# Heads grouped by halves of the rows and sums of exponentials on GpSimd, in an attention and feed-forward kernel ordered by a written list

## The chip, the core and the metric

The kernel runs on one core of a Trainium2 chip. The metric is the device time of one execution in microseconds (us), lower being better. Several runs are given by their median. The engines are called PE (the matrix engine; its weight loads are shown apart as PEld), DVE (the vector engine), ACT (the scalar engine), POOL (GpSimd) and SP (the queue that issues the stores).

## What is computed

The reference has two parts. The first is an attention over 32 memory slots, for 8 batches, 8 heads, 576 tokens and a head size of 64. The second is a feed-forward product, whose input is the attention's output with the heads side by side.

```python
a = exp(phi - max(phi, axis=2));  a = a / (sum(a, axis=2) + 1e-9)
k_m = einsum('bhsm,bhsd->bhmd', a, k);  v_m = einsum('bhsm,bhsd->bhmd', a, v)
attn = softmax(q @ k_m^T / 8);  x = attn @ v_m          # heads merged: (4608, 512)
out = ((x @ w_a) * (x @ w_b)) @ w_out                    # 512 -> 1536 -> 512
```

The sum below a slot's exponentials is a sum over tokens: 32 slots, each with its own sum, for each head and batch.

## The kernel before

**Layout.** A batch's q, k, v and phi are loaded as 128 partitions by four slabs (`hp`). Partitions 0 to 63 of slab `hp` hold head 2·hp, partitions 64 to 127 head 2·hp+1, and each partition has nine tokens of its head. So a head is named by the half of the rows that it lies in (`r`, 0 or 1) and its slab. A group `g` is four heads, `j` = 0 to 3, whose 32 slots each lie side by side in 128 partitions. `head(g, j)` says which heads make a group: it crosses the halves, so that each group takes two heads from either half.

**Batches 2 to 7.** `exp0` and `exp1` (L260) take exponentials of phi on ACT, two slabs each. `kv` (`kv_sums`, L286) multiplies the exponentials with k, v and a block of ones in 72 products of 64 rows, 32 columns and 192 moving columns, on eight tiles of the array at once. The block of ones gives each slot's sum. `km` (`take_kv`, L313 and L318) divides by the sums into a tile of six 128x128 squares (`rep`), in which the means stand repeated, since the scores and the folds read them from the rows in which the head's data lie. `kvt` (L326, L327) turns the six squares on PE and copies them out. `sc` (L375) makes the scores from the turned means and the transposed q (`qt0` to `qt3`, L269). `e0` and `e1` take their exponentials, `den`, `nr` or `ed`, `sm`, `tn`, `ad` normalise. `v0` to `v2` (`fold`, L447) multiply the value means into w_a and w_b, and `x0` to `x2` (L460) copy these out.

**Batches 0 and 1** do the same in smaller steps (`ks`, `kt`, `vs`, `vt`, `s`, `hv`, `hx`, L340 to L361), because their inputs still arrive.

**Feed-forward.** `a` and `b` (`up_half`, L621) are two products each with 288 moving columns: batch, one of twelve blocks of the 1536 columns, half of the tokens. ACT copies the first (L625), DVE multiplies it with the second (L628). The down product is made for two blocks of 128 tokens at once by seven products instead of eight, from sums of the inputs (`h` on POOL, `g` on DVE, L534) and of the weights (`T` on POOL, `V` on DVE, L517). A `d` with a number is that many of its 756 matmuls of 256 columns (L550).

**Order.** Nothing is reordered by the compiler. A string, `PLAN`, lists all steps, and every engine runs its own instructions in the order in which the list issues them. `F` and `f` with a number are matmuls of 512 and 128 columns on zeros that keep PE busy. `p`, `k`, `v`, `q`, `w` and `o` are loads, all issued from POOL: phi, k, v and q of a batch, columns of w_a and w_b, rows of w_out. `M` is a POOL memset of the block of ones of odd batches, `O` fills the matrix that `den` multiplies with.

Tiles for phi and q have two buffers each, so batch b+2's phi takes the place of batch b's. k and v have one tile for even batches and one for odd.

Of the kernel before, what the change touches and what calls it, by code (L numbers as in the profile page):

```python
# [13 lines left out]
P = 128  # L14
# [11 lines left out]
f3 F1 O 0exp0 f1 f1 F2 p1 f2 f6 F7 w0:256 f2 f1 k1 f1 F3 0exp1 F5 f2 0qt0 q1.0 0ks0 0ks1 F5 0kt0 0qt1 M F2 0s0  # L26
w256:512 0qt2 0kt1 0e0 0den00 0qt3 0s1 0e1 F4 0den01 1exp0 0vs0 q1.1 0vt0 v1 0vs1 1exp1 F6 0nr00 0den10 0vt1
0den11 0hv0a 0hx0a 0nr10 0hv0b 0hx0b 0nr11 a0.1.0 b0.1.0 a0.0.0 F4 0nr01 1ks0 1ks1 b0.0.0 0hv1a 0hx1a 1kt0 1kt1
1qt0 1qt1 a0.0.1 a0.2.1 F1 b0.0.1 1s0 a0.1.1 0hv1b 1qt2 1qt3 0hx1b 1s1 1e0 1e1 b0.2.1 1den0 a0.2.0 b0.1.1 b0.2.0
1den1 1vs1 1vs0 1vt1 1nr0 1vt0 1nr1 a0.3.1 a0.3.0 1hv1b 1hx1b 1hv0b 1hv0a 1hx0a w512:1024 1hx0b b0.3.1 b0.3.0  # L30
1hv1a 0v1a 1hx1a 0x1a a1.0.0 a1.1.1 a1.1.0 a1.0.1 b1.0.0 b1.1.1 b1.1.0 a1.3.0 b1.0.1 a1.3.1 b1.3.0 b1.3.1 a0.5.0
0v1b 1v1a w1024:1536 0x1b 1x1a a1.2.0 1v1b 0v2a 1x1b o1 0x2a a0.7.1 b0.5.0 b1.2.0 b0.7.1 a0.7.0 b0.7.0 o5 a1.5.0
a1.2.1 b1.2.1 b1.5.0 a0.4.0 a0.6.0 b0.4.0 a0.4.1 a1.4.0 b0.6.0 b1.4.0 a0.9.1 0v2b 1v2b 1v2a 0x2b 1x2b a1.5.1
b0.4.1 1x2a b0.9.1 a0.8.0 a1.4.1 b1.5.1 o2 a0.5.1 a0.6.1 b0.8.0 a0.9.0 b0.6.1 b0.9.0 b1.4.1 a1.7.1 b0.5.1 b1.7.1
a0.8.1 b0.8.1 o0 a1.7.0 a0.10.0 b1.7.0 b0.10.0 a0.11.0 a1.9.0 o3 o4 b0.11.0 g0.0 b1.9.0 a1.6.1 k2 a1.6.0 p2 h0.3
a0.11.1 b1.6.1 b0.11.1 a1.8.1 a0.10.1 b1.6.0 v2 b1.8.1 g0.1 T01 a1.8.0 T00 V20 q2 T21 d1 2exp0 a1.9.1 d3 b0.10.1
p3 a1.10.0 d2 V10 g0.2 V11 d1 b1.9.1 2exp1 d1 a1.11.1 k3 d1 q3 T31 T30 d1 b1.10.0 b1.8.0 d1 b1.11.1 d4 h1.0 d2
2kv d4 2km d3 a1.11.0 d10 a1.10.1 2qt0 3exp0 d1 2kvt d2 h1.1 d1 2qt1 d12 2qt2 d3 2qt3 b1.10.1 g1.2 b1.11.0 v3 d1
2sc 2e0 d1 g1.3 d3 g2.0 d3 2e1 d1 2den0 h2.1 d8 p4 d8 2nr0 2den1 g2.2 2v0 2x0a 2x0b d2 2nr1 d10 2v1 d5 2x1a 3qt0
d3 g2.3 d3 2x1b d1 a2.3.0 a2.2.0 b2.3.0 b2.2.0 q4 k4 v4 a2.5.0 3exp1 b2.5.0 d2 3qt1 d4 a2.0.0 b2.0.0 d3 h3.0  # L40
a2.1.0 a2.4.0 2v2 3kv 3qt3 2x2a 3qt2 b2.1.0 2x2b d2 a2.11.1 a2.6.0 d4 3km a2.8.0 d1 q5 b2.4.0 d3 b2.6.0 d2 4exp0
d5 b2.11.1 d5 h3.1 d2 b2.8.0 a2.11.0 3kvt d2 a2.8.1 a2.7.1 b2.8.1 d2 a2.9.0 b2.7.1 3sc 3e1 3e0 g3.3 d1 b2.11.0
4qt0 a2.7.0 d2 a2.5.1 b2.5.1 b2.7.0 h3.2 3den0 d1 3nr0 4qt3 d1 b2.9.0 d2 a2.0.1 4qt2 a2.10.0 b2.0.1 p5 a2.4.1
b2.10.0 d1 k5 a2.10.1 d3 b2.10.1 d3 h4.0 4exp1 d1 a2.2.1 b2.4.1 3den1 d4 3v1 3x1a 4kv 3v0b 3x1b d3 3x0b d1 3nr1
d6 4km0 h4.1 a2.6.1 b2.2.1 a2.9.1 4qt1 a2.1.1 3v0a 3v2 d1 3x0a d2 3x2a d2 b2.6.1 3x2b d4 a3.9.0 d4 a3.5.0 d2
4km1 h4.2 b2.9.1 d1 a2.3.1 4kvt d1 b2.1.1 d1 b2.3.1 d2 5qt0 4sc a3.11.0 d1 h4.3 b3.5.0 5qt2 d5 4e1 d1 4e0 d1 v5
d6 b3.9.0 a3.0.0 g5.0 d1 h5.1 d3 4ed b3.11.0 d1 a3.3.0 d2 a3.10.1 b3.0.0 h5.2 5exp0 4sm0 q6 a3.1.0 d1 b3.3.0 d4
a3.3.1 d2 p6 d2 b3.10.1 a3.8.1 h5.3 d1 b3.3.1 b3.1.0 a3.6.0 b3.6.0 a3.7.0 a3.10.0 b3.8.1 d1 a3.1.1 b3.7.0 5qt1
d2 a3.8.0 a3.2.0 b3.10.0 d3 5exp1 a3.4.0 d1 b3.8.0 b3.1.1 d2 b3.2.0 k6 b3.4.0 4v0a 5kv 4x0a d1 a3.2.1 5km0
a3.4.1 5km1 d3 h6.0 h6.1 b3.2.1 d1 a3.9.1 d3 a3.5.1 d1 b3.4.1 b3.9.1 d5 4v0b 4x0b 4tn0 4v1 d1 h6.3 d3 4x1a d1  # L50
4x1b d2 a3.11.1 5kvt d1 p7 4sm1 a3.7.1 h6.2 d1 v6 d3 a3.6.1 d2 b3.5.1 b3.11.1 d1 5qt3 4v2 d4 4tn1 a3.0.1 d7 4x2a
4ad 6exp0 d1 b3.0.1 d6 4x2b b3.7.1 a4.11.0 b3.6.1 d1 a4.9.0 6exp1 d1 6qt0 b4.11.0 a4.7.0 a4.4.0 d4 b4.9.0 k7 d1
5sc 5e1 d1 5e0 d1 a4.0.0 d1 b4.4.0 d1 b4.0.0 a4.2.0 b4.2.0 d1 b4.7.0 d3 6qt1 d2 a4.4.1 d2 q7 a4.1.1 b4.4.1 5v0
5x0a 5x0b 6kv 5v1 h7.0 5x1a d3 6km0 a4.10.1 d1 5ed 6km1 d2 h7.3 h7.1 b4.1.1 h7.2 g8.0 d1 5x1b d2 h8.1 d1 a4.6.1
d4 b4.6.1 d4 a4.8.0 a4.5.0 5sm0 d1 v7 d1 h8.2 b4.10.1 a4.8.1 b4.8.0 a4.3.1 b4.5.0 d2 6qt3 d7 5v2 d2 5x2a d2
a4.1.0 d2 b4.3.1 7qt0 a4.3.0 d1 5x2b d1 b4.8.1 d1 7qt2 d1 b4.3.0 a4.5.1 d2 a4.10.0 b4.1.0 d2 6kvt 7exp0 d2 5tn0
d3 5sm1 a4.0.1 b4.5.1 d1 6qt2 d2 b4.0.1 d1 a4.6.0 d3 a4.7.1 d5 h8.3 d1 b4.10.0 d1 7exp1 d2 5tn1 d1 7qt1 a4.11.1
d3 6sc d5 6e1 d5 a4.2.1 d1 b4.7.1 d1 b4.6.0 5ad d1 a4.9.1 d1 h9.0 d1 b4.2.1 d3 6e0 b4.11.1 d1 b4.9.1 d1 a5.2.0
d1 a5.2.1 6ed g9.1 d1 b5.2.0 6v0a 6x0a 6v0b 7kv 6x0b b5.2.1 a5.11.0 b5.11.0 a5.8.0 a5.9.0 b5.8.0 h9.2 d1 7km0 d1
a5.3.0 d1 h9.3 d2 b5.9.0 b5.3.0 d2 a5.6.0 d1 g10.0 d1 h10.1 b5.6.0 a5.3.1 h10.3 d4 b5.3.1 d2 a5.1.0 d5 7qt3 d4  # L60
a5.7.0 d1 7km1 a5.7.1 b5.7.1 d9 b5.7.0 a5.5.0 d3 b5.1.0 d4 6sm0 b5.5.0 d3 a5.0.0 a5.1.1 d1 a5.10.0 d1 b5.0.0
7kvt d3 a5.0.1 d2 h10.2 b5.1.1 b5.0.1 d6 b5.10.0 a5.11.1 a5.10.1 6sm1 a5.4.0 d2 6v1 b5.10.1 6x1a d3 b5.4.0 d2
6x1b d1 b5.11.1 d1 a5.5.1 a5.9.1 6v2 6x2b b5.5.1 d1 6tn1 d1 a5.8.1 d1 6tn0 a5.6.1 d1 6x2a a5.4.1 d1 6ad b5.9.1
d4 7sc d1 7e1 7e0 b5.6.1 d2 b5.4.1 b5.8.1 a6.7.0 d1 7ed a6.9.0 7v0a 7v1 g11.0 d2 7x1a d2 g11.1 d2 a6.10.0 h11.3
h11.2 d1 h12.0 d3 7x0a 7sm0 a6.0.0 d2 b6.7.0 d2 b6.10.0 d4 b6.9.0 d5 a6.3.0 d7 a6.11.0 b6.11.0 b6.0.0 d1 a6.2.0
d5 b6.2.0 d1 a6.8.0 d1 b6.3.0 d1 7x1b d1 a6.5.0 h12.1 a6.10.1 b6.5.0 d4 7sm1 d4 h12.2 d3 a6.6.1 d2 g12.3 d3
b6.8.0 d6 a6.4.1 d3 b6.4.1 a6.9.1 d2 7tn1 b6.10.1 d1 7tn0 d3 7ad d2 b6.6.1 a6.2.1 a6.3.1 d1 a6.1.0 d1 b6.3.1
b6.2.1 d2 b6.9.1 d5 a6.8.1 a6.4.0 b6.1.0 b6.8.1 a6.11.1 b6.4.0 a6.6.0 b6.6.0 h13.0 a6.1.1 h13.1 a6.5.1 b6.11.1
d1 b6.5.1 d1 7v0b 7v2 d1 7x0b 7x2a a6.0.1 b6.1.1 d1 7x2b b6.0.1 d1 g13.2 d1 a6.7.1 d2 a7.11.0 d5 a7.6.0 a7.7.0
d7 g13.3 d1 b6.7.1 b7.6.0 b7.11.0 a7.0.0 d1 b7.7.0 d2 a7.2.0 d1 b7.0.0 d10 a7.1.0 a7.4.1 a7.3.0 d1 b7.2.0 b7.3.0  # L70
b7.1.0 d1 a7.10.1 a7.4.0 h14.0 h14.3 d7 b7.4.1 d2 a7.5.0 a7.10.0 g14.1 b7.5.0 d1 b7.4.0 b7.10.1 a7.5.1 a7.3.1
b7.5.1 d1 b7.10.0 a7.8.0 d1 a7.9.1 b7.3.1 d1 h14.2 a7.1.1 d1 b7.8.0 b7.9.1 a7.8.1 a7.9.0 d2 b7.9.0 d3 h15.0 d1
h15.1 d2 a7.2.1 b7.1.1 d3 a7.7.1 d15 b7.8.1 d3 g15.2 d4 a7.0.1 g15.3 d11 b7.0.1 d3 b7.2.1 d1 a7.11.1 d3 b7.7.1
d1 a7.6.1 d2 b7.11.1 d10 b7.6.1 g16.0 d6 g16.1 d5 g16.2 d1 g17.0 d11 h16.3 d8 h17.1 d24 h17.3 d13 g17.2 d28
# [4 lines left out]
def kernel(  # L79
# [167 lines left out]
    def head(g, j):  # L247

        jj = j ^ g
        return jj % 2, 2 * g + jj // 2  # L250

    def units(b):

        u = {}
# [16 lines left out]
        def slot_sums(z):  # L271
            if z == 0:
                t["es"] = kvs[b][:, 2, 0, 0:2 * NHP * M].bitcast(F32).rearrange("p (c m) -> p c m", m=M)
            nc.vector.tensor_reduce(out=t["es"][:, 2 * z:2 * z + 2], in_=t["exp"][:, 2 * z:2 * z + 2].rearrange("p c i m -> p c m i"),
                                    axis=mybir.AxisListType.X, op=ALU.add)
# [30 lines left out]
        def take_kv(gs=range(2)):  # L306

            if gs[0] == 0:
                t["rep"] = mid.tile([P, 6, P], F16, name="rep")
                t["rphi"] = small.tile([P, 2], F32, name="rphi")  # L310
            for g in gs:
                pkv, bank = t["pkv"][g]
                nc.vector.reciprocal(out=t["rphi"][:, g:g + 1], in_=pkv[:, 2 * D:2 * D + 1])  # L313
                km = pkv[:, 0:D].rearrange("p (d e) -> p e d", e=2).unsqueeze(2).to_broadcast([P, 2, 4, 32])
                vm = pkv[:, D:2 * D].unsqueeze(1).to_broadcast([P, 2, D])
                for out, x in ((t["rep"][:, 2 * g:2 * g + 2].rearrange("p e (z d) -> p e z d", z=4), km),
                               (t["rep"][:, 4 + g].rearrange("p (z d) -> p z d", z=2), vm)):
                    nc.vector.tensor_scalar(out=out, in0=x, scalar1=t["rphi"][:, g:g + 1], scalar2=None, op0=ALU.mult)  # L318
                banks.free(bank)

        def kv_transpose():
# [3 lines left out]
            for x in range(6):  # L325
                nc.tensor.transpose(out=pT[:, x, :], in_=t["rep"][:, x], identity=ident)  # L326
# [136 lines left out]
        def one(f, *a):  # L463
            return lambda: f(*a)
# [221 lines left out]
```

## Time and profile before

| | |
|---|---|
| time, median of 3 runs | 237.14 us (237.03 to 237.19) |
| time of the profiled execution | 237.06 us |
| its span | 235.4 us |
| PE busy | 226.6 us, 96% |
| DVE busy | 186.9 us, 79% |
| ACT busy | 152.6 us, 65% |
| POOL busy | 132.0 us, 56% |

The span is what the profiler saw of the program, from its first instruction to its last. Some 1.7 us of the execution's time lie outside it. Busy shares are means over the whole span. A PE matmul's busy time contains the latency of its result, and matmuls overlap; the distance from one start to the next says more of its cost.

### The profile page before, as it was taken

What the parts mean: (1) busy time and instruction counts of PE and PEld (TensorE: products, weight loads), DVE (VectorE), ACT (ScalarE), POOL (GpSimd) and SP (SyncE); (2) the same over time, 40 slices, a digit from 0 to 9 for tenths busy, and PEclk for the clock granted to TensorE, in tenths of its full rate; (3) what the DMA queues carried; (4) which work ended last, traced back from release to release, by engine and by line L of the source; (5) the groups of instructions that cost most, each with busy time, mean ns of one, the idle gap of its engine ahead of it and who ended that gap; (6) DMA issues with size and microseconds to landing.
All of it is one profiled execution on the core that took longest, in us unless ns stands there. A gap on an engine that the chain in (4) does not pass through costs nothing.

```text
span 235.4 us, 7727 instructions
## 1 busy us (share of the span) xinstructions
PE 226.6 (96%) x3075; PEld 171.4 (73%) x3075; DVE 186.9 (79%) x454; ACT 152.6 (65%) x398; POOL 132.0 (56%) x117
## 2 busy tenths in 40 slices
PE   7988899999999999999999999999999999999993
PEld 4534466788877887888777778788668887888882
DVE  4536699999988889898897998987798687776842
ACT  2265598875697699667787856754884757464330
POOL 6784423895695647776979380665209205535251
PEclk9999999999999999999999999999999999999999
DMA  6999999999999979399699582303030412041264
GB/s 232 235 252 203 207 207 207 205 259 258 214 249 214 198 170 238 66 176 214 117 227 206 133 138 54 92 1 92 1 76 16 92 45 49 1 93 43 57 148 111
DMA packets 25748, 34.12 MB, mean 145 GB/s; under 512 B 2000, under 2 KB 19792, under 8 KB 25712
## 3 DMA queue, kind: packets, MB, share of 16 engines
q0 software_dynamic: 19248, 23.14, 54.0%
q1 hardware_dynamic: 5952, 9.70, 15.6%
q10 hardware_dynamic: 512, 0.79, 1.0%
q8 instruction: 24, 0.39, 0.6%
q14 instruction: 12, 0.10, 0.1%
HBM read 42.47 MB, written 9.44 MB: 221 GB/s over the span
## 4 chain that ended last, share of the span: by engine, by line
PE 86%; DMA 7%; POOL 3%; DVE 1%; issue 0%
PE py L550 21%; PE pb L621 20%; PE pa L621 20%; PE pv L550 10%; PE pva L447 5%; PE px L550 5%; DMA q_sb<-in_q_dram 5%; DMA ht<-in_k_dram 2%; PE pkv L286 2%; PE pscore L375 1%; POOL kv_sb L639 1%; PE pT L326 1%; PE pD L398 1%; POOL wa_sb L159 1%; DVE kv_sb L217 1%; POOL wb_sb L160 1%
## 5 line engine op out<-in xcount | busy, mean ns | idle before, releaser
L625 ACT CAST a_sb<-pa 128x288 f16<-128x288 f32 x192 | 72.3, 407 | 38.1 <-PE pa L621 30.6
L628 DVE TENSOR_TENSOR ht<-a_sb,pb 128x288 f16<-128x288 f16 x192 | 80.1, 447 | 19.6 <-PE pb L621 12.0
L621 PEld LDWEIGHTS <-vab 128*128 128x128 f16 x768 | 73.8, 98 | 19.1 <-issue 3.0
L621 PE MATMUL pb<-A,vab 128*128 128x288 f16 x384 | 71.9, 286 | 0.0
L621 PE MATMUL pa<-A,vab 128*128 128x288 f16 x384 | 71.3, 286 | 0.6 <-DVE A L409 0.4
L534 POOL TENSOR_TENSOR h_sums<-ht 128x768 f16<-128x768 f16 x22 | 36.0, 1640 | 36.5 <-DVE ht L628 36.4
L550 PEld LDWEIGHTS <-h_sums 128*128 128x128 f16 x432 | 41.8, 98 | 9.0 <-issue 1.5
L550 PEld LDWEIGHTS <-ht 128*128 128x128 f16 x324 | 31.0, 98 | 8.5 <-issue 3.5
L460 ACT CAST vab<-pva 128x512 f16<-128x512 f32 (+1 forms) x60 | 31.3, 570 | 7.2 <-PE pva L447 6.8
L550 PE MATMUL py<-w_sums,h_sums 128*128 128x256 f16 x216 | 35.4, 273 | 0.0
L534 POOL TENSOR_TENSOR h_sums<-h_sums,ht 128x768 f16<-128x768 f16 x13 | 21.3, 1639 | 15.1 <-DVE h_sums L534 7.1
L460 DVE CAST vab<-pva 128x512 f16<-128x512 f32 (+1 forms) x44 | 26.8, 635 | 2.9 <-PE pva L447 2.8
L534 POOL TENSOR_TENSOR h_sums<-ht,h_sums 128x768 f16<-128x768 f16 x11 | 18.1, 1643 | 11.0 <-PE pa L621 5.9
L550 PE MATMUL pv<-w_sums,h_sums 128*128 128x256 f16 x108 | 19.3, 273 | 0.0
L557 ACT ACTIVATE u<-py 128x256 f32<-128x256 f32 x36 | 14.0, 390 | 8.1 <-PE py L550 6.2
L550 PE MATMUL px<-wo_sb,ht 128*128 128x256 f16 x108 | 19.0, 273 | 0.0
L550 PE MATMUL py<-wo_sb,ht 128*128 128x256 f16 x108 | 18.9, 273 | 0.0
L550 PE MATMUL py<-w_sums,ht 128*128 128x256 f16 x108 | 18.5, 273 | 0.0
L550 PE MATMUL pv<-wo_sb,h_sums 128*128 128x256 f16 x108 | 18.5, 273 | 0.0
L269 DVE STREAM_TRANSPOSE qT<-q_sb 128x288 f32<-128x288 f32 x32 | 14.5, 465 | 2.1 <-DMA q_sb<-in_q_dram 2.1
L260 ACT ACTIVATE exp_sb<-phi_sb 128x576 f16<-128x576 f32 x16 | 10.8, 687 | 6.0 <-DMA phi_sb<-in_phi_dram 6.0
L211 PE MATMUL pw<-warm 128*128 128x512 f16 (+1 forms) x59 | 13.2, 382 | 1.3 <-DVE warm L180 1.3
(69 smaller groups left out, 247.5 us busy)
## 6 DMA issues: line engine op xcount, KB each, us to landing
out_dram<-o_sb SPq DMA_DIRECT2D x68, 128.0 KB, 2.4
phi_sb<-in_phi_dram POOLq DMA_DIRECT2D x8, 576.0 KB, 7.1
kv_sb<-in_v_dram POOLq DMA_DIRECT2D x8, 576.0 KB, 9.2
kv_sb<-in_k_dram POOLq DMA_DIRECT2D x7, 576.0 KB, 9.9
q_sb<-in_q_dram POOLq DMA_DIRECT2D x6, 576.0 KB, 10.7
wo_sb<-in_moe_w_out_dram POOLq DMA_DIRECT2D x6, 256.0 KB, 15.8
q_sb<-in_q_dram POOLq DMA_DIRECT2D x4, 288.0 KB, 9.7
wa_sb<-in_moe_w_a_dram POOLq DMA_DIRECT2D x2, 512.0 KB, 15.3
```

What stands on the lines that cost most here:

```text
L211: nc.tensor.matmul(pw[:, :cols], warm[:, :P], warm[:, :cols], start=True, stop=True)
L260: nc.scalar.activation(out=t["exp"][:, 2 * z:2 * z + 2, :, :], in_=phis[b][:, 2 * z:2 * z + 2, :].rearrange("p c (i m) -> p c i m", m=M), ...
L269: nc.vector.transpose(out=t["qT"][:, hp, :].bitcast(F32), in_=qs[b][:, hp, :].bitcast(F32))
L286: nc.tensor.matmul(t["pkv"][g][0][32 * j:32 * j + 32, 0:n], t["exp"][64 * r:64 * r + 64, hp, i, :], kvs[b][64 * r:64 * r + 64, 0:3 - given ...
L447: nc.tensor.matmul(t["pva", lo, z][g][0][32 * j:32 * j + 32, 0:hi - lo], t["kvT"][64 * r:64 * r + 64, 4 + g, M * j:M * j + M], w_sbs[z][64 ...
L460: engine_copy(out=vabs[b][z][:, g, lo:hi], in_=pva[:, 0:hi - lo])
L534: engine.tensor_tensor(out=out, in0=in0, in1=in1, op=op)
L550: nc.tensor.matmul(po, lhs[:, i], rhs[:, i], start=first and i == 0, stop=i == KH - 1, skip_group_check=not first)
L557: nc.scalar.mul(out=x, in_=po, mul=scale)
L621: nc.tensor.matmul(ps, vabs[b][x][:, g, P * i:P * (i + 1)], attn[b][:, g, HALF * hf:HALF * (hf + 1)], start=(g == 0), stop=(g == 1))
L625: nc.scalar.copy(out=a_sbs[b, i, hf], in_=ps)
L628: nc.vector.tensor_tensor(out=ht[:, i, t0:t0 + HALF], in0=a_sbs.pop((b, i, hf)), in1=ps, op=ALU.mult)
```

## The change

Four things change.

1. From batch 2 on a group is made by `straight`: group 0 is the four heads of partitions 0 to 63, group 1 those of partitions 64 to 127. Both groups then share three squares, one group in either half, where there were six. `take_kv` writes half the columns, `kv_transpose` makes three products and a copy of 384 columns. Batches 0 and 1 keep `crossed`, and their turned means move to a pool of their own.
2. The block of ones leaves the product of batches 2 to 7. A step `ps0` (`slot_sums`) adds the exponentials over the nine tokens of each partition in four POOL instructions of 512, 256, 128 and 128 elements, in 32-bit, into the phi tile that the exponentials came from. Eight small products of 32-bit operands, with one moving column, finish the sum over partitions at the end of `kv_sums` (the branch `given`, which stood in the kernel but was not used).
3. `slot_sums` as it stood (two DVE reductions into the block of ones) is gone; no list called it.
4. The list is written anew. The number of `a`, `b` and `d` steps is the same. POOL's `h` go from 46 to 42 and DVE's `g` from 26 to 30, `T` from 5 to 6 and `V` from 3 to 2. `F` go from 40 to 47 and `f` from 19 to 6.

```diff
-    def head(g, j):
+    def crossed(g, j):
         jj = j ^ g
         return jj % 2, 2 * g + jj // 2
+    def straight(g, j):
+        return g, j
     def units(b):
+        side = b < 2
+        head = crossed if side else straight
...
-        def slot_sums(z):
-            if z == 0:
-                t["es"] = kvs[b][:, 2, 0, 0:2 * NHP * M].bitcast(F32).rearrange("p (c m) -> p c m", m=M)
-            nc.vector.tensor_reduce(...)
+        def slot_sums():
+            e = t["exp"]
+            f = phis[b].rearrange("p c (i m) -> p c i m", m=M)
+            for out, in0, in1 in ((f[:, :, 0:4], e[:, :, 0:4], e[:, :, 4:8]), (f[:, :, 0:2], f[:, :, 0:2], f[:, :, 2:4]),
+                                  (f[:, :, 0], f[:, :, 0], f[:, :, 1]), (f[:, :, 0], f[:, :, 0], e[:, :, 8])):
+                nc.gpsimd.tensor_tensor(out=out, in0=in0, in1=in1, op=ALU.add)
+            t["es"] = f[:, :, 0]
...
         def take_kv(gs=range(2)):
-                t["rep"] = mid.tile([P, 6, P], F16, name="rep")
+                t["rep"] = mid.tile([P, 3, P], F16, name="rep")
...
-                km = pkv[:, 0:D].rearrange("p (d e) -> p e d", e=2).unsqueeze(2).to_broadcast([P, 2, 4, 32])
-                vm = pkv[:, D:2 * D].unsqueeze(1).to_broadcast([P, 2, D])
-                for out, x in ((t["rep"][:, 2 * g:2 * g + 2].rearrange("p e (z d) -> p e z d", z=4), km),
-                               (t["rep"][:, 4 + g].rearrange("p (z d) -> p z d", z=2), vm)):
+                km = pkv[:, 0:D].rearrange("p (d e) -> p e d", e=2).unsqueeze(2).to_broadcast([P, 2, 2, 32])
+                half = slice(D * g, D * (g + 1))
+                for out, x in ((t["rep"][:, 0:2, half].rearrange("p e (z d) -> p e z d", z=2), km),
+                               (t["rep"][:, 2, half], pkv[:, D:2 * D])):
...
         def kv_transpose():
-            t["kvT"] = mid.tile([P, 6, P], F16, name="kvT")
-            pT = banks.tile([P, 6, P], F16, name="pT")
-            for x in range(6):
+            t["kvT"] = mid.tile([P, 3, P], F16, name="kvT")
+            pT = banks.tile([P, 3, P], F16, name="pT")
+            for x in range(3):
...
         def sums(g, x):
-                t["kvT"] = mid.tile([P, 6, P], F16, name="kvT")
+                t["kvT"] = consts.tile([P, 6, P], F16, name=f"kvT{b}")
...
         def scores(gs):
-                                t["kvT"][row:row + 32, 2 * g + dh, M * j:M * j + M],
+                                t["kvT"][row:row + 32, (2 * g if side else 0) + dh, M * j:M * j + M],
...
         def fold(lo, hi, zs):
-                            t["kvT"][64 * r:64 * r + 64, 4 + g, M * j:M * j + M],
+                            t["kvT"][64 * r:64 * r + 64, 4 + g if side else 2, M * j:M * j + M],
...
-            u[f"ps{z}"] = one(slot_sums, z)
+        u["ps0"] = slot_sums
```

Of the new list, the start and the stretches in which batches 2 to 4 have their sums:

```diff
+p1 F2 F2 M f2 0exp0 F2 F4 O F3 f3 F2 F6 f1 0exp1 0ks0 0ks1 F3 0kt0 0qt0 0qt1 0s0 k1 F1 0qt2 0e0 w0:256 F8 0kt1
+0vs0 0qt3 0den00 0vs1 q1.0 1exp0 0s1 w256:512 F3 0vt0 0vt1 0e1 0den10 0nr00 0den01 F2 0den11 q1.1 v1 0nr01 1exp1
+1ks0 0hv0a 0nr10 0hx0a 1kt0 0nr11 1ks1 F5 0hv0b a0.1.0 1qt0 a0.0.1 1qt1 w512:1024 0hx0b 1s0 0hv1a 0hx1a a0.0.0
+b0.1.0 b0.0.0 1kt1 b0.0.1 0hv1b 1e0 0hx1b 1qt3 1den0 1qt2 a0.1.1 a0.2.0 b0.1.1 a0.3.1 1nr0 1s1 1e1 b0.2.0 a0.2.1
+a0.3.0 b0.2.1 1den1 b0.3.0 1vs1 1vs0 1vt1 1vt0 w1024:1536 1nr1 b0.3.1 1hv0b 1hv0a 1hv1b 1hx1b 1hx0a 1hv1a 0v1a
...
+b1.9.0 a1.8.1 a1.6.0 b1.6.0 2exp0 a0.10.1 d1 b1.8.1 a1.10.0 v2 g0.1 d1 T01 a1.9.1 a1.8.0 V20 T00 d4 g0.2 V11
+b0.10.1 q2 d1 T21 b1.10.0 d2 2exp1 p3 d1 T10 d1 a1.11.1 d1 b1.9.1 d3 q3 2ps0 b1.8.0 d2 b1.11.1 d7 k3 d1 T30 d2
+T31 d1 g1.0 2kv 2km d1 F4 d5 2qt0 2qt3 2qt1 2qt2 a1.10.1 g1.1 v3 d2 3exp0 a1.11.0 2kvt b1.11.0 b1.10.1 d2 g1.2
+d16 2sc d1 q4 d1 g1.3 2e0 2e1 d9 g2.0 d1 2den0 2den1 d1 g2.1 3exp1 2nr0 2nr1 d1 g2.3 d7 g2.2 d1 2v0 d6 2x0b d1
+p4 d1 3qt0 d6 3qt2 d2 2x0a d1 2v1 2x1a d8 2x1b a2.2.0 3ps0 3qt3 a2.3.0 b2.3.0 a2.0.0 h3.0 d2 b2.2.0 d1 k4 d1
+b2.0.0 d6 h3.1 d3 2v2 3kv 2x2a 2x2b d1 a2.8.0 d1 a2.5.0 a2.4.0 d2 v4 3qt1 3km p5 b2.5.0 b2.8.0 d1 a2.1.0 q5 d7
...
+a2.7.1 a2.7.0 4qt3 d1 4qt2 4exp0 d6 4exp1 d1 b2.8.1 b2.7.0 b2.7.1 d1 3den0 a2.0.1 h3.3 d3 b2.0.1 4qt1 a2.11.0 d1
+a2.1.1 d2 3nr0 a2.10.0 b2.11.0 d2 b2.10.0 d2 3den1 d2 a2.10.1 d2 q6 g4.0 3v1 3x1b 4ps0 d1 b2.1.1 d3 a2.4.1 d1
+a2.6.1 h4.1 d1 b2.10.1 a2.2.1 d1 3x1a d6 v5 d1 a2.9.1 3v0b 3x0b 4kv 4km0 d1 h4.2 d5 4km1 d1 3v2 3v0a 3nr1 3x2a
```

The start of the list before, for comparison:

```diff
-f3 F1 O 0exp0 f1 f1 F2 p1 f2 f6 F7 w0:256 f2 f1 k1 f1 F3 0exp1 F5 f2 0qt0 q1.0 0ks0 0ks1 F5 0kt0 0qt1 M F2 0s0
-w256:512 0qt2 0kt1 0e0 0den00 0qt3 0s1 0e1 F4 0den01 1exp0 0vs0 q1.1 0vt0 v1 0vs1 1exp1 F6 0nr00 0den10 0vt1
-0den11 0hv0a 0hx0a 0nr10 0hv0b 0hx0b 0nr11 a0.1.0 b0.1.0 a0.0.0 F4 0nr01 1ks0 1ks1 b0.0.0 0hv1a 0hx1a 1kt0 1kt1
-1qt0 1qt1 a0.0.1 a0.2.1 F1 b0.0.1 1s0 a0.1.1 0hv1b 1qt2 1qt3 0hx1b 1s1 1e0 1e1 b0.2.1 1den0 a0.2.0 b0.1.1 b0.2.0
-1den1 1vs1 1vs0 1vt1 1nr0 1vt0 1nr1 a0.3.1 a0.3.0 1hv1b 1hx1b 1hv0b 1hv0a 1hx0a w512:1024 1hx0b b0.3.1 b0.3.0
```

## The prediction

> **What bounds the kernel now.** I read the page's busy shares and slices first, then the table of stretches, then the chain of waits, and last single steps in the order of time.
>
> ```profile
> PE 226.6 (96%) x3075; PEld 171.4 (73%) x3075; DVE 186.9 (79%) x454; ACT 152.6 (65%) x398; POOL 132.0 (56%) x117
> PEclk9999999999999999999999999999999999999999
> ```
>
> ```profile
> 24.00:30.00 6.00, 5.33 (x93) 2.76 (x97) 3.92 (x11) 3.90 (x13) 2.10 (x3) 1.00 1.22 207
> 30.00:42.00 12.00, 11.82 (x219) 7.91 (x220) 11.88 (x32) 11.11 (x31) 3.60 (x5) 1.00 1.24 207
> 42.00:60.00 18.00, 18.00 (x237) 14.19 (x235) 17.27 (x44) 12.64 (x35) 14.53 (x12) 1.00 1.19 240
> 60.00:100.00 40.00, 40.00 (x634) 31.17 (x632) 35.28 (x86) 32.17 (x84) 26.97 (x23) 1.00 0.94 192
> 150.00:200.00 50.00, 50.00 (x589) 39.14 (x588) 41.59 (x97) 33.68 (x89) 22.04 (x15) 1.00 0.21 49
> ```
>
> The columns are the stretch, its length, the busy time of PE, PEld, DVE, ACT and POOL, the granted clock, the DMA share and GB/s. From 42 us on PE has no hole, at the full clock (1.00). So from there any start-to-start time that leaves PE shortens the run, and any that is added lengthens it; other engines count only if PE comes to wait for them. POOL is busy 14.53 of 18 us from 42 to 60, which is where it may become late, and only 22.04 of 50 from 150 on. Before 42 us DMA is full (share over 1.2), and the start is a matter of landings:
>
> ```profile
> 11.78 2.03 POOL kv_sb L639
> 15.17 11.87 DMA q_sb<-in_q_dram
> 29.97 0.79 PE pk L340 x72
> ```
>
> The chain puts 2.03 us on the memset `M`. It should not be believed: the load behind it landed 11.87 us after its issue, since the queue was full of earlier bytes. `M`'s move to an earlier place is worth nothing, and `p1`'s too (its bytes follow v's in either list).
>
> Prices of single steps, start to start:
>
> ```profile
> 56.22 0.94 PE L286 MATMUL pkv<-kv_sb,exp_sb 64*32 64x192 f16 x72
> 57.09 0.28 PE L550 MATMUL py<-w_sums,h_sums 128*128 128x256 f16 x1
> 59.56 0.50 PE L326 MATMUL pT<-ident,rep 128*128 128x128 f16 x6
> 59.89 0.27 PE L550 MATMUL px<-wo_sb,ht 128*128 128x256 f16 x1
> 60.00 0.27 PE L550 MATMUL py<-w_sums,ht 128*128 128x256 f16 x1
> 13.81 1.04 PE L211 MATMUL pw<-warm 128*128 128x512 f16 x4
> 14.69 0.29 PE L398 MATMUL pD<-E,ones 128*128 128x288 f16 x1
> ```
>
> So a `kv` takes 0.87 us, six turning products 0.33, a down matmul of 256 columns 0.11 (0.43 ns a column), four fills of 512 columns 0.88. By the same count an up half is 0.245.
>
> **Part by part.** All sums are against the profiled execution, 237.06 us, 0.08 below the median of 237.14.
>
> *Turning.* Three products fewer, 0.33/2 = 0.17, six batches: 1.0 us off PE. The shorter DVE work (rows of 484 and 342 ns become like the 342 and 284 ns rows, the copy of 555 ns becomes shorter; some 0.6 us a batch) lies beside PE and is set at nothing; were DVE the bound it would be a gain.
>
> *Width.* 72 products on eight tiles are nine waves; 64 columns fewer are 64 x 0.43 = 27 ns a wave, 0.25 us a batch: 1.5 us off PE.
>
> *Eight small products.* No row shows 32-bit operands. Below, at the spacing of the other `kv` products (0.87/72 = 12 ns) with half of it hidden: 0.05 us a batch. Above, one after another like the turning products (56 ns): 0.45. I take 0.2, nearer to the `kv` row, since they too lie on eight tiles, but with a weight load that nothing hides. Six batches: 1.2 us on PE (0.3 to 2.7).
>
> The Trainium skill, "FP8 and Floating Point Precision", TensorE Precision Notes, says that true 32-bit products take four passes. By that the eight would be 32 small ones, and as the 32 score products take 0.41 us here, the sum would be 1.3 us later; no run here shows it yet.
>
> *Grouping by halves.* Scores and folds keep their number, tiles and columns, and either order uses all tiles at once. Nothing.
>
> *Sums on POOL.* 1024 elements a batch. POOL's two-input rows (768 elements 1640 ns, 576 1279, 640 1265) give 2.0 to 2.2 ns an element, 2.2 us, and four starts at 0.08 make some 2.4. Bounds: 2.0, and 4.0 if 32-bit results cost more. In all 14.4 us on POOL, while four `h` leave it and a `T` comes (net -4.9): 132 becomes about 141 of 235.
>
> The Trainium skill, "GPSIMD Engine Reference", Engine selection, speaks against this part: two-input elementwise work and sums along the free dimension belong on VectorE, GpSimd being about 2x slower. Here it is 3x (`h_sums` takes 1640 ns on POOL, 545 on DVE). By the rule one would lose 14.4 us of engine time; as neither engine is the bound, I count only PE's waits.
>
> PE waits if `ps0` is late, for the small products stand in PE's order before all that follows. Counting PE's steps in the list: from `2exp1` to `2kv` four up halves and 20 down matmuls, 3.2 us, and 0.6 of `kv` itself; against that the exponentials (0.69), some 0.1 to 0.5 of ACT's backlog and 2.4: 0.2 to 0.6 spare. Batch 3: 8.3 us of steps from `2nr0` on, against 1.3 us of lag as before, two `nr` (2.6), `p4` (0.8), 2.4: 1.8 spare with `kv`'s 0.6. Batch 4: 6.0 from `3nr0`, against 1.7 of lag, 1.3, `q6` 0.75, 2.4: 0.5 spare. Batches 5 to 7: over 1.5. So nothing, up to the point where a sum takes about 2.9 us.
>
> phi's loads `p4` to `p7` now wait on POOL's queue for the sums and the small products of two batches before. Those lie 1 us (`p5`) to over 7 us earlier in the list, so nothing. `q`, `k` and `v` change places by one load, 1.5 to 3 us in a stream that is 10 to 30 us ahead of use after 65 us: nothing.
>
> *A fill at 58 us.* `F4` stands in the new list behind `2km`: 0.9 us on PE, certain. It covers a wait rather than making one: `T30` and `T31` now come behind `ps0` on POOL, ending some 7.1 to 7.5 us after `2exp1`, and PE's 40th down matmul, which needs `T31`, has 7.1 us of steps before it with the fill. Left out, PE would wait about as long.
>
> *One more changeover* between tile shapes (`3v1` now stands apart): 0.15.
>
> *The start.* The weights w0:256 land 2.8 us later (k1 goes ahead of them), w256:512 (24.3), q1.1 (27.04) and v1 (29.9) as now. Fills in between cost nothing, as there is no input. When v's sums of batch 1 begin at 29.97, twelve up halves are done; the new list puts fifteen before them. Followed through: two up halves and `1s0` before 24.3; then eight steps without a hole to 27.6; `1s1` waits for q1.1 and two transposes, 27.95; `1den1` waits for ACT, 29.95; v's sums at 30.45. Three up halves gained (0.75), 0.5 given back: 0.2 us earlier. DVE and ACT are nearly full from 30 to 42, so I allow 0.8 earlier to 0.8 later.
>
> Sum: -1.0 - 1.5 + 1.2 + 0.9 + 0.15 - 0.2 = -0.45, so 236.6 us.
>
> **Rivals.**
>
> *Small products nearly free, and the start gains its most* (0.3 for 1.2, -0.8 for -0.2): -1.95 + 0.45 = about -1.9, 235.2 us. For it: all other products on eight tiles issue within nanoseconds. Against: nothing hides their weight loads.
>
> *PE waits for POOL.* If a sum takes 4.0 us, batch 2 is late by 1.2 and batch 4 by 1.1, and the rest not: 2.3 on 236.6, 238.9 us, slower. It decides from 2.9 us a sum. For it: POOL's 81% between 42 and 60 us, and a first step from 16-bit into 32-bit, which no row has. Against: 576, 640 and 768 elements agree per element, one of them with a 32-bit input.
>
> *Leaving out the block of ones saves nothing,* because the small products cost what it did or more (0.45 for 0.25): +1.5 on the forecast, 238.1 us, slower.
>
> **How the numbers follow.** Forecast 0.42, split 0.24 faster and 0.18 within the bound, since it stands close to it; cheap products 0.22; POOL late 0.19; dear products 0.17, of which 0.03 within. A measurement of this kernel can tell about 0.2% (0.47 us) from no change. Faster 0.46, same 0.21, slower 0.33. The forecast's own range is 235.9 to 237.3. The range for 8 in 10 takes in most of the others: 235.0 to 239.0.
>
> **What would show it.** Right: `pkv` bursts of about 0.8 us start to start with the eight; three turning products in 0.17; POOL's four sums together near 2.4 us; PE without a hole after 42 us except about the fill; the 40th down matmul near 61 us. Wrong: a PE gap that ends with POOL's release in a `kv`, a burst over 0.87 us, a hole between 30 and 42 us whose releaser is DVE, ACT or a weight load.

## The result and the profile after

The changed kernel is slower: 238.53 us (238.49 to 238.59, 4 runs) against 237.16 us (237.03 to 237.49, 4 runs beside it). The ratio is 1.0054, its 95% interval 1.0036 to 1.0072. The forecast was 236.6 us, 1.9 us too low, and on the wrong side; the range for 8 in 10, 235.0 to 239.0, takes the result in. The profiled execution took 238.54 us, with a span of 236.8 us.

First the page of the changed kernel, in the same lines as before: busy time and share of each engine, and the granted clock.

```profile
PE 227.5 (96%) x3147; PEld 170.5 (72%) x3147; DVE 188.3 (79%) x457; ACT 151.9 (64%) x398; POOL 143.9 (61%) x138
PEclk9999999999999999999999999999999999999998
```

The shares say next to nothing: PE is busy 96% in both kernels. The table of stretches (columns as before) says where to look.

```profile
30.00:42.00 12.00, 11.70 (x223) 7.58 (x222) 11.63 (x30) 9.94 (x28) 3.65 (x5) 1.00 1.24 206
42.00:60.00 18.00, 17.81 (x236) 13.57 (x235) 16.83 (x42) 11.96 (x33) 16.10 (x15) 1.00 1.19 241
60.00:100.00 40.00, 38.99 (x621) 29.93 (x620) 35.58 (x87) 30.82 (x81) 32.13 (x32) 1.00 1.06 215
```

Before, PE had no hole from 42 us on. Now it idles 0.19 us between 42 and 60 and 1.01 us between 60 and 100 (40.00 less 38.99). In the latter stretch POOL went from 26.97 to 32.13 us. The chain of waits shows one break there: PE stops, there is nothing but DVE's copy `vab`, and PE goes on.

```profile
90.06 0.26 PE pb L631 x2
...
90.58 0.69 DVE vab L470
...
91.31 0.40 PE pa L631 x2
```

The single steps of DVE and of POOL at that place, in the order of time (start, duration, engine, line, operation), show why `vab` was late:

```profile
88.44 2.22 DVE L544 TENSOR_TENSOR h_sums<-ht 128x768 f16<-128x768 f16 x1
90.58 0.68 DVE L470 CAST vab<-pva 128x512 f16<-128x512 f32 x1
```

```profile
88.25 0.79 POOL L151 DMA_DIRECT2D q_sb<-in_q_dram  x1
89.07 1.16 POOL L284 TENSOR_TENSOR phi_sb<-exp_sb 128x512 f32<-128x512 f16 x1
```

`g4.0`, a sum on DVE whose median is 0.55 us, took 2.22. It was issued at 88.44, while POOL issued `q6`, and it ended at 90.66, 0.43 us after POOL's first slot sum of batch 4 (90.23). PE's up half needed the copy that stood behind it, and started 1.17 us late. So the new POOL sums held up PE, but not by being late themselves: by holding up DVE.

The smaller hole, before 60 us, is of the same kind. DVE, then POOL, then PE:

```profile
50.23 1.13 DVE L544 TENSOR_TENSOR h_sums<-ht 128x768 f16<-128x768 f16 x1
```

```profile
50.16 0.78 POOL L139 DMA_DIRECT2D phi_sb<-in_phi_dram  x1
50.97 1.89 POOL L527 TENSOR_TENSOR w_sums<-wo_sb,w_sums 128x768 f16<-128x768 f16 x1
```

```profile
51.78 0.40 PE L631 MATMUL pa<-A,vab 128*128 128x288 f16 x2 [0.18 <-DVE ht L638]
```

This is `g0.0`, beside the load `p3` with the sum `T10` ready behind it. Before, the same sum took 0.56 us beside the same load (50.38, the load from 50.31 on), behind which two more loads stood. PE's start before this one (51.31) lies 0.47 us ahead, 0.35 more than the product takes.

The places that the prediction named, in PE's single steps around batch 2's `kv`:

```profile
57.62 0.80 PE L296 MATMUL pkv<-kv_sb,exp_sb 64*32 64x128 f16 x72
58.43 0.27 PE L307 MATMUL pkv<-one_cs,phi_sb 64*32 64x1 f32 x16
58.64 0.28 PE L560 MATMUL py<-w_sums,h_sums 128*128 128x256 f16 x1
58.76 1.03 PE L212 MATMUL pw<-warm 128*128 128x512 f16 x4
60.87 0.33 PE L336 MATMUL pT<-ident,rep 128*128 128x128 f16 x3
61.04 0.65 PE L631 MATMUL pb<-A,vab 128*128 128x288 f16 x4
```

From 57.62 to 58.64 is 1.02 us for `kv` with its small products (0.92 in the other five batches), where 0.87 stood before and 0.8 was predicted; a burst over 0.87 was named as a sign of being wrong. The three turning products take 0.17, as predicted. The fill takes 0.86 (58.76 to 59.62). The 40th down matmul starts at 61.95, not near 61. POOL's four slot sums of this batch:

```profile
54.94 1.15 POOL L284 TENSOR_TENSOR phi_sb<-exp_sb 128x512 f32<-128x512 f16 x1 [1.36 <-ACT exp_sb L267]
56.16 1.26 POOL L284 TENSOR_TENSOR phi_sb<-phi_sb 128x256 f32<-128x256 f32 x2
57.50 0.43 POOL L284 TENSOR_TENSOR phi_sb<-phi_sb,exp_sb 128x128 f32<-128x128 f32 x1
```

They take 2.99 us (54.94 to 57.93), not 2.4, and end 0.50 us before the first small product. No small product waited for POOL in this kernel.

### The profile page after: what moved, and what is told of

It reads as the page before. It is cut to its first block, busy times and chain, and to the rows that moved or that the text cites. A ratio compares the mean times of both kernels' runs of the same rounds, so it can differ in the third digit from the quotient of the medians.

```text
span 236.8 us, 7895 instructions
## 1 busy us (share of the span) xinstructions
PE 227.5 (96%) x3147; PEld 170.5 (72%) x3147; DVE 188.3 (79%) x457; ACT 151.9 (64%) x398; POOL 143.9 (61%) x138
## 4 chain that ended last, share of the span: by engine, by line
PE 86%; DMA 7%; DVE 3%; POOL 1%; issue 1%; ACT 0%; DVEq 0%
PE py L560 21%; PE pb L631 20%; PE pa L631 20%; PE pv L560 10%; PE pva L457 5%; PE px L560 5%; DMA q_sb<-in_q_dram 5%; DMA ht<-in_k_dram 2%; PE pkv L296 2%; DVE kv_sb L218 1%; PE pscore L385 1%; PE pD L408 1%; PE pT L336 0%; PE pkv L307 0%; PE pw L212 0%
## 5 line engine op out<-in xcount | busy, mean ns | idle before, releaser
L635 ACT CAST a_sb<-pa 128x288 f16<-128x288 f32 x192 | 73.2, 411 | 39.4 <-PE pa L631 30.0
L638 DVE TENSOR_TENSOR ht<-a_sb,pb 128x288 f16<-128x288 f16 x192 | 79.3, 445 | 21.7 <-PE pb L631 11.4
L544 POOL TENSOR_TENSOR h_sums<-ht 128x768 f16<-128x768 f16 x20 | 32.6, 1637 | 26.4 <-DVE ht L638 26.4
L544 POOL TENSOR_TENSOR h_sums<-h_sums,ht 128x768 f16<-128x768 f16 x11 | 18.0, 1641 | 10.8 <-PE pb L631 7.7
L560 PE MATMUL pv<-wo_sb,h_sums 128*128 128x256 f16 x108 | 18.0, 272 | 0.0
L560 PE MATMUL py<-w_sums,ht 128*128 128x256 f16 x108 | 17.1, 272 | 0.0
L212 PE MATMUL pw<-warm 128*128 128x512 f16 (+1 forms) x53 | 14.3, 422 | 1.3 <-DVE warm L181 1.3
L276 DVE STREAM_TRANSPOSE qT<-q_sb 128x288 f32<-128x288 f32 x32 | 13.8, 457 | 1.0 <-DMA q_sb<-in_q_dram 1.0
```

Of the source, the lines that this page charges most:

```text
L212: nc.tensor.matmul(pw[:, :cols], warm[:, :P], warm[:, :cols], start=True, stop=True)
L276: nc.vector.transpose(out=t["qT"][:, hp, :].bitcast(F32), in_=qs[b][:, hp, :].bitcast(F32))
L544: engine.tensor_tensor(out=out, in0=in0, in1=in1, op=op)
L560: nc.tensor.matmul(po, lhs[:, i], rhs[:, i], start=first and i == 0, stop=i == KH - 1, skip_group_check=not first)
L635: nc.scalar.copy(out=a_sbs[b, i, hf], in_=ps)
L638: nc.vector.tensor_tensor(out=ht[:, i, t0:t0 + HALF], in0=a_sbs.pop((b, i, hf)), in1=ps, op=ALU.mult)
```

## The experiments

"Collision" is the theory that a DVE sum of two tensors in SBUF can't run while a POOL sum does. "Cover" is the theory that the fill hides a wait that would be there anyway. Each kernel was timed in turn with the kernel before on the same chip; ratios are to that.

**One DVE sum put earlier.** The changed kernel with `g4.0` in front of the stretch where POOL sums:

```diff
-... b2.10.0 d2 3den1 d2 a2.10.1 d2 q6 g4.0 3v1 3x1b 4ps0 ...
+... b2.10.0 g4.0 d2 3den1 d2 a2.10.1 d2 q6 3v1 3x1b 4ps0 ...
```

> One step moved in the changed kernel: DVE's token sum g4.0 stands right after b2.10.0, so that DVE asks for it while POOL still runs the multiplication 3nr0, not between the load q6 and POOL's slot sums 4ps0. Collision theory (a DVE sum of two 16-bit SBUF tiles and a POOL sum do not run at the same time; g4.0 took 2218 ns instead of 551 and PE stood for 1.2 us at 90.0 us behind it): the hole goes, 238.5 - 1.2 = 237.3 us, g4.0 near 550 to 1100 ns. Rival (PE's hole comes from the copies and PSUM banks there, g4.0 only lies beside it): the hole stays, 238.5 us.

Measured: 237.76 us, ratio 1.0025 (1.0016 to 1.0035). The hole at 90 us is gone, and 0.77 us come back, less than the 1.2 expected. Right behind the place PE is 1.25 us earlier than in the changed kernel, at its last start 0.97; what takes the rest was not followed up. Even here the sum met a POOL step, the tail of `3nr0`: it took 0.96 us from 87.69, to 0.42 us after that step's end:

```profile
87.69 0.96 DVE L544 TENSOR_TENSOR h_sums<-ht 128x768 f16<-128x768 f16 x1
```

```profile
86.95 1.28 POOL L419 TENSOR_TENSOR A<-E,R 128x576 f16<-128x576 f16 x1 [2.28 <-ACT R L417]
```

**The sums issued ahead of the load.** `g4.0` stays behind `3nr0`; `q6` goes behind `4ps0`:

```diff
-... d2 q6 g4.0 3v1 3x1b 4ps0 d1 ...
+... d2 g4.0 3v1 3x1b 4ps0 q6 d1 ...
```

> The changed kernel with POOL's load q6 behind the slot sums 4ps0 instead of before them; g4.0 keeps its place. If DVE's token sum only waits for the one POOL sum that runs when it asks (some 1.1 us), it ends near 90.0 instead of 90.66 us and PE's hole shrinks from 1.2 to about 0.5 us: 237.9 us. If POOL keeps DVE out until its queue of ready sums is empty (3.0 us): hole of 2.5 us, 239.9 us. If the load in front of the sums was what held DVE: no hole, 237.3 us.

Measured: 237.7 us, 1.0023 (1.0014 to 1.0033). DVE's sum, and the POOL sum that it meets:

```profile
88.28 1.40 DVE L544 TENSOR_TENSOR h_sums<-ht 128x768 f16<-128x768 f16 x1
```

```profile
88.11 1.16 POOL L284 TENSOR_TENSOR phi_sb<-exp_sb 128x512 f32<-128x512 f16 x1
```

The sum ends at 89.68, 0.41 us after POOL's first (89.27). Without the load in between it waits 0.85 us instead of 1.67, and PE's hole is 0.35 us instead of 1.17: the first of the three forecasts. So the load counted in the changed kernel, since a slot sum that could have run stood behind it.

**Without the fill.** `F4` behind `2km` is left out, nothing else:

> The fill F4 of the changed list left out, nothing else. Cover theory (POOL ends the weight sum T31 at 61.9 us, the first matmul that needs it comes 0.1 us later, so PE would wait without the fill): 238.5 us, unchanged within 0.2, and a hole of 0.7 to 0.9 us before the matmul that reads T31. Rival (the fill is plain extra work): 238.5 - 0.86 = 237.6 us.

Measured: 238.6 us, 1.0059 (1.0046 to 1.0072), the changed kernel's time. PE's step behind the hole, with the idle time and its releaser in brackets:

```profile
62.01 0.49 PE L560 MATMUL py<-w_sums,ht 128*128 128x256 f16 x3 [0.85 <-POOL w_sums L527]
```

From the start before it (60.88) to this one is 1.13 us, 1.02 more than the product takes, where the fill cost 0.86: `T31` comes late on POOL. The cover theory holds, and the fill isn't what costs, but POOL's order.

**The halves alone.** The list of before and the block of ones kept; only the grouping by `straight` with three turning products is new:

> The list of before with the block of ones kept and no sums on POOL; of the change only the grouping by halves and the three turning products. Theory (turning is the one part that pays, 6 x 0.168 us, and scores and folds cost the same in either grouping): 237.16 - 1.0 = 236.15 us. Rival (four products in a row on the same half of the rows run worse in kv, scores or folds): 237.2 us or more, with longer bursts of those lines.

Measured: 236.11 us, 0.995 (0.9938 to 0.9962). This is better than both kernels; of those here that compute the whole only the one with the new start added (236.01 us, below) is level with it. PE's time from 30 us to its last start goes down by 1.05 us, of which the turning products give 1.00 (2.01 to 1.01). Between 60 and 100 us it also frees DVE: 34.44 us of busy time in that stretch of its table instead of 35.28.

**Fewer columns in `kv`.** On top of the halves alone, two kernels with narrower products, 128 columns (k and ones) and 64 (ones alone):

```diff
-            n = (3 - given) * D
+            n = 2 * D                                                        # the second kernel: 1 * D
-                            kvs[b][64 * r:64 * r + 64, 0:3 - given, hp, D * i:D * (i + 1)],
+                            kvs[b][64 * r:64 * r + 64, 0:3:2, hp, D * i:D * (i + 1)],     # the second: 2:3
```

> As e3 (halves only, list of before, 236.11 us), but the 72 products of a kv take 128 moving columns, k and ones; v is left out (the value means are replaced by the key means). No small products. Issue theory (after the first 32 products of a burst the next ones start every 8.3 ns whatever their width, as the changed kernel's bursts show): about 0.07 us a batch off the burst, 236.11 - 0.4 = 235.7 us. Width theory of the prediction: 0.25 us a batch, 234.6 us.

> As e6 with 64 moving columns, the block of ones alone; k and v are left out (all means are ones). Issue theory: 72 starts of 8.3 ns are 0.6 us and the changeover 0.1, so at most 0.17 us a batch under e3's 0.87: 235.1 us. Width theory: 0.5 us a batch, 233.1 us.

Measured: 235.89 us, 0.9949 (0.9935 to 0.9963), and 235.54 us, 0.9931 (0.9919 to 0.9944). The theory of the width, which the prediction went by (234.6 and 233.1 us here), falls; the issue theory (235.7 and 235.1) is nearer. Batch 2's `kv` and the next step on PE, first with 128 columns, then with 64 (with 192 they start at 56.17 and 57.04 in the halves alone):

```profile
56.40 0.80 PE L295 MATMUL pkv<-kv_sb,exp_sb 64*32 64x128 f16 x72
57.14 0.28 PE L559 MATMUL py<-w_sums,h_sums 128*128 128x256 f16 x1
```

```profile
56.34 0.75 PE L295 MATMUL pkv<-kv_sb,exp_sb 64*32 64x64 f16 x72
57.02 0.28 PE L559 MATMUL py<-w_sums,h_sums 128*128 128x256 f16 x1
```

Start to start this is 0.87 us with 192 columns, 0.74 with 128 and 0.68 with 64. Added over the six batches 5.03, 4.54 and 4.39 us: the first 64 columns bring 0.50 us, the next 0.15. These are the bursts alone: PE's last start comes only 0.11 and 0.30 us earlier than in the halves alone. The starts inside a burst tell why. With 192 columns, in batch 2, eight products start within some 25 ns, and the next eight begin 59 ns after the last of them: some 82 ns a wave, which is 192 columns at 0.43 ns, so the array sets the pace. With 128 columns the first waves are shorter by the 27 ns that the prediction counted, but that lasts for 24 or 32 products only. With 128 as with 64 columns almost all that follow start 8.3 ns after one another, whatever their width: 67 ns for eight. 40 to 48 of the 72 go by that.

**The block of ones kept.** The changed kernel, its list without the six `ps0`, so that the products have 192 columns again and no small ones:

> The changed kernel with the block of ones instead of the slot sums on POOL and the small products; its list otherwise unchanged. Theory (sums cost 1.2 us by the collision at 90.0 us and 0.04 us a batch on PE, since 72 products of 128 columns and the sixteen small passes take 717 + 203 ns where 72 of 192 columns took 881): 238.5 - 1.2 - 0.2 = 237.1 us, and kv bursts of 0.87 us. Rival (the new list as such is the slower one): 238.5 us. Width theory of the prediction (0.25 us a batch saved by narrower products): only 238.5 - 1.2 + 0.3 = 237.6 us.

Measured: 240.23 us, 1.0127 (1.0106 to 1.0149), far off the expected 237.1. Taking steps from POOL made this list slower. DVE, then POOL, then PE at the place:

```profile
53.11 3.30 DVE L544 TENSOR_TENSOR h_sums<-h_sums,ht 128x768 f16<-128x768 f16 x1
```

```profile
53.58 0.75 POOL L143 DMA_DIRECT2D kv_sb<-in_k_dram  x1
54.34 1.65 POOL L527 TENSOR_TENSOR w_sums<-wo_sb,w_sums 128x768 f16<-128x768 f16 x1
```

```profile
56.47 0.50 PE L560 MATMUL py<-w_sums,h_sums 128*128 128x256 f16 x3 [1.01 <-DVE h_sums L544]
57.87 0.38 PE L560 MATMUL py<-w_sums,h_sums 128*128 128x256 f16 x2 [0.66 <-DVE w_sums L527]
```

In the changed kernel the same DVE sum, at the same 53.11 and beside the same load, takes 0.55 us: there the next POOL step was `2ps0`, which still waited for ACT. Here `T30` could run, and stood behind two loads, `q3` (from 52.81) and `k3`; DVE's sum waited for all three and ended at 56.41, 0.42 us after `T30`. Three holes of PE, the third behind ACT, make 2.57 us. The profiled run took 240.81 us, since after them the granted clock is 0.5 for 3.4 us; the runs at a mean clock of 0.999 to 1.000 took 239.46 to 239.66. The kernel does not price the small products, then, but it is the clearest case of the collision.

**Both repairs at once.** `g4.0` earlier, no fill, and `T31` given to DVE as `V31` behind `2km`:

> As e1 (g4.0 earlier, 237.76 us), and the second half of the fourth weight sum (T31) goes from POOL to DVE, right behind 2km, with the fill F4 left out. Theory (POOL's queue at 55 to 62 us, lengthened by the slot sums, costs PE the 0.86 us of the fill and 0.2 behind it): 237.76 - 1.06, less some 0.3 for the turn of the means that DVE now makes later: 237.0 us. Rival (the place of the weight sums does not matter, PE waits there for the means): 237.7 us.

Measured: 237.8 us, 1.0024 (1.0014 to 1.0034), no better than the first repair alone. PE's steps:

```profile
60.95 0.83 PE L560 MATMUL py<-w_sums,ht 128*128 128x256 f16 x6 [0.36 <-DVE o_sb L571]
63.45 0.79 PE L385 MATMUL pscore<-qT,kvT 32*32 32x288 f16 x32 [0.36 <-DVE kvT L337]
```

The wait went from POOL to DVE. `V31` took 0.83 us (59.72 to 60.55, again until 0.42 after a POOL sum's end at 60.13) and pushed the transposes of q behind it. Each hole is 0.53 us beyond the time of the product ahead of it; together they cost 1.06 us, no less than the fill's 0.86 us.

**The new start alone.** The halves alone, with the new list up to `1vs1` and the old one behind it:

> As e3 (halves only, block of ones, 236.11 us), but the list begins as the new one up to the v sums of batch 1 (1vs1) and goes on as the list of before, without the steps already done. It shows what the new start is worth by itself. Reading of the two traces (fifteen up halves instead of twelve are issued by 30 us, 0.7 us of PE's work): 236.1 - 0.7 = 235.4 us, or 235.9 if only the 0.2 us of the prediction remains. Rival (DVE and ACT, full from 30 to 42 us, take the lead back): 236.1 us.

Measured: 236.01 us, 0.9963 (0.9949 to 0.9976), against 236.11 for the halves alone: no gain that can be told. By 30 us fifteen up halves have started instead of twelve, by 34 us 19 against 18.5, by 38 us 30 in both. The stretch from 30 to 42 us with the new start, in which the halves alone have PE busy for 11.82 us:

```profile
30.00:42.00 12.00, 11.49 (x217) 7.69 (x216) 11.60 (x30) 10.25 (x29) 3.61 (x5) 1.00 1.24 206
```

PE loses 0.33 us more to holes there. One, 0.33 us at 31.87, ends with DVE's copy of batch 1's turned means, and DVE is busy 97% of the stretch.

**The sums in the old list.** The changed kernel's code in the list of before, with each `ps0` behind its `exp1`:

> All of the change except the new order: the list of before, with each batch's slot sums right behind its second exponential. Theory (the order of before has no room for 3.0 us of sums on POOL at batch 2): PE waits about 1.1 us for the sums in 2kv and 1.4 us for the fourth weight sum behind them, and kv costs 0.04 us a batch more than with the block of ones, so 236.1 + 2.7 = 238.8 us, more where sums on POOL and DVE's token sums meet. Rival (the sums themselves are harmless and the new list is what costs): 236.3 us.

Measured: 249.51 us, 1.0507 (1.0466 to 1.0548), where 238.8 was expected. Two of the six runs had a mean clock of 1.000 (247.35 and 247.52 us), the others of 0.982 to 0.993 (248.84 to 250.55). The waits of PE by releaser (us in all, times, longest), in the profiled execution of 247.52 us:

```profile
PE pkv L306 <- POOL phi_sb L283: 6.6, 4, 3.3
PE py L559 <- POOL w_sums L526: 1.6, 1, 1.6
```

The small products wait for POOL's sums in four of the six batches. The longest wait ends at 97.40; on POOL there:

```profile
92.75 1.66 POOL L543 TENSOR_TENSOR h_sums<-ht 128x768 f16<-128x768 f16 x1
94.35 1.16 POOL L283 TENSOR_TENSOR phi_sb<-exp_sb 128x512 f32<-128x512 f16 x1
...
96.92 0.43 POOL L283 TENSOR_TENSOR phi_sb<-phi_sb,exp_sb 128x128 f32<-128x128 f32 x1
```

Here the rival "PE waits for POOL" is true, at 3.0 us a batch of sums: they stand behind the older work on POOL's queue. The new list is what keeps them off the path.

## Why the prediction was right or wrong, point by point

All figures in the table are PE time, start to start, from the traces of before and after; gains are negative.

| term | predicted, us | measured, us |
|---|---|---|
| turning | -1.0 | -1.0 (2.01 to 1.00) |
| width of `kv` | -1.5 | -0.6 (5.03 to 4.40) |
| small products | +1.2 | +1.10 |
| fill | +0.9 | +0.86 |
| changeover | +0.15 | +0.1 |
| DVE's `g4.0` behind POOL | none | +1.17 |
| DVE's `g0.0` behind POOL's load, PE at 51.31 | none | +0.35 |
| start | -0.2 | -0.4: 0.73 gained by 30 us, 0.33 lost in two waits by 32.6 |
| sum | -0.45 | +1.6 |

From 30 us on PE's starts take 202.40 us instead of 200.98; the gain of the three up halves that are done before then is in this difference of +1.4, and 0.2 of the sum stays unassigned. The medians differ by 1.37.

**Turning** and **grouping** were right: the halves alone gained 1.07 us by the medians, and PE kept its steps otherwise. That DVE's shorter work is worth nothing was right too, since 0.84 us less DVE between 60 and 100 us brought nothing beyond the turning.

**The width** is a term whose mechanism was half right and whose size was off by 0.9 us. "72 products on eight tiles are nine waves; 64 columns fewer are 64 x 0.43 = 27 ns a wave" holds for the first three or four waves. Behind them the products start 8.3 ns apart, eight in 67 ns where 192 columns took 82, and a width below that no longer counts. So 0.50 us for the first 64 columns in the experiment (0.6 in the changed kernel) against 1.5.

**The small products** were right in size, 0.18 us a batch against 0.2. The trace records sixteen passes for the eight, so two for each product. By the rule of the Trainium skill that the prediction quoted ("FP8 and Floating Point Precision", TensorE Precision Notes: four passes) there would be 32; neither the records nor the time, 1.10 us for the six batches, agree with that here. With the width, `kv` costs 0.47 us more instead of 0.3 less: the rival "leaving out the block of ones saves nothing" came true. Its reason was not that the products were dear, but that the columns were cheap.

**The step that failed most** is the sentence "as neither engine is the bound, I count only PE's waits" about the sums on POOL. PE's waits for POOL's results were counted and, but for 0.09 us at 61.95 behind `T31`, are not there, though the sums take 3.0 us and not 2.4 (the small steps cost more than their elements: 128 elements 0.43 us, 512 1.15). What was left out is the second way in which POOL can hold PE up: POOL holds DVE, and PE needs DVE. That term stood at nothing and measured 1.5 us (1.17 and 0.35), the larger part of the 2.05 us by which the sum misses. Every DVE sum of two SBUF tensors that was issued while a POOL sum ran ended only after that sum, in every run. In the trace of before this happened to one of 29: the one at 226.29 us took 1.17 us, where the median is 0.55. It was there to be seen. DVE, then POOL, before:

```profile
226.29 1.17 DVE L534 TENSOR_TENSOR h_sums<-ht,h_sums 128x768 f16<-128x768 f16 x1
```

```profile
225.40 1.64 POOL L534 TENSOR_TENSOR h_sums<-ht 128x768 f16<-128x768 f16 x1
```

So was the price: with POOL at 80% of a stretch, and DVE's `g` rising from 26 to 30, meetings could be expected to get likelier.

The Trainium skill says this in "SBUF — State Buffer", Who interferes with whom: a VectorE instruction with two inputs in SBUF contends with a GpSimd instruction that reads SBUF, one of them waits for the whole of the other, and the order of issue decides which. That one waits for the other the runs show too (`g4.0` ended 0.41 to 0.43 us after the POOL step that it met, in five kernels). On the order they agree only in part: in the changed kernel `g4.0` started 0.63 us ahead of POOL's sum, which stood behind a load (88.44 against 89.07), and still ended behind it. The prediction weighed the sentence that GpSimd is slower, and not this one, which spoke against the change.

**The fill** was right as a price and as a cover: without it the time is the same. But a cover is not a reason to pay. The wait that it covers ends with `T31` (62.01, without the fill), which stands behind the sums on POOL; giving `T31` to DVE made two waits of one.

**The start** was set at -0.2, with more room either way. The lead by 30 us was larger (0.73 us), and was not kept; the larger of the two waits, at 32.59, ends with DVE, which the prediction had named as a sign. In the new start with the old continuation nothing measurable is left; how much of it the changed kernel keeps wasn't separated.

**The moved memset `M`** was set at nothing and was nothing for the end. It did hold DVE: the first cast of k, beside it on POOL, took 2.65 us (5.78 to 8.43) instead of 0.75, while `M` ran from 5.77 to 7.81.

**The rival "PE waits for POOL"** gave 238.9 us, near the result, by another mechanism. That was luck. The mechanism is shown in the old list, at 3.0 us of sums, and not in the new one.

**The rival "small products nearly free"** did not come true (1.10 us against its 0.3). Its recorded sum has a slip: its terms add up to -1.95, 235.1 us, and the +0.45 beside them has no place there.

## What to carry to other kernels

Before moving elementwise work to GpSimd, look up which DVE steps read two tensors from SBUF, and where they will stand beside it: each meeting costs DVE up to a whole POOL step, and more where POOL's step waits behind a load. Columns taken from many small matmuls pay only as long as the array sets their pace; read the starts inside one burst before multiplying columns by a rate. Where a change has independent parts, run each alone: here the part that gained 1.07 us was hidden under the rest, which cost 2.4.

## What the runs showed of the hardware

- A DVE sum of two f16 tensors in SBUF (128x768, 0.55 us alone) that meets a two-input POOL step ends 0.41 to 0.46 us after that step's end. Steps of DVE with one input in PSUM don't care: `ht<-a_sb,pb` has a median of 447 ns in the changed kernel, beside POOL's two-input steps and without.
- A load that POOL issues does not hold DVE by itself (0.55 us at 53.11 in the changed kernel). With a POOL sum behind it that could run, it did: DVE's sum took 2.22, 3.30 and 1.13 us in three places. In the last of these (50.23) DVE went ahead of the POOL sum once the load was over, in the others behind it; what decides stays open.
- Products of 64 rows and 32 columns on eight tiles start 3 to 4 ns apart at first, and mostly 8.3 ns apart after the first 24 to 32 of a burst, with 64 and with 128 moving columns.
- After three holes of PE within four microseconds (2.57 us in all) the granted clock fell to 0.5 for 3.4 us, in some runs of that kernel, which then took 1.3 us longer. One hole of 1.17 us in the changed kernel did not bring it down, nor did one of 3.32 us in the profiled run of the sums in the old list.
